# A mixture-of-experts and gated-MLP kernel: fold and scale product a step later, transposes spread through the expert stage

## The chip, the cores and the metric

The kernel runs on one core of a Trainium2 chip. The metric is the time of one execution on the device, in microseconds (us). The core has five engines that work side by side, each through its own queue in order: PE (TensorE, matrix products and transposes into PSUM), DVE (VectorE), ACT (ScalarE), POOL (GpSimd) and SP (SyncE, which issues the DMAs here).

## The reference

Three stages follow each other: an attention between tokens and a few state rows, a soft mixture of experts, and a gated MLP. Cut to what matters here:

```python
attn = concat([softmax(x @ state.T) @ state, softmax(state @ x.T) @ x])   # 8 x 544 rows of 512 = 4352 tokens
logits = attn @ phi                                  # 32 slots: 8 experts with 4 slots each
slot_in = softmax(logits, over tokens).T @ attn
slot_out[e] = relu(slot_in[e] @ w1[e]) @ w2[e]       # 8 experts, 512 -> 1024 -> 512
y = softmax(logits, over slots) @ slot_out           # 4352 x 512
g = y @ w_gate                                       # 512 -> 1536
out = (g * sigmoid(g) * (y @ w_val)) @ w_out         # 1536 -> 512
```

## The kernel before, in words

Every order in it is written by hand: the engines run their instructions in the order in which the Python code emits them.

**Attention stage.** A string of operation names (ORDER) sets it. Neither it nor its code is touched.

**Expert stage** (from L1102). The experts run in two groups g of four. `expert_1` multiplies the slot inputs with w1, `expert_r` applies the relu, `expert_h` transposes the result, `expert_2` multiplies with w2, and `expert_o` copies the outputs out of PSUM (L692) and transposes them by a small product (L694) into the stack ST. Between them lies side work, in generators of which `some(gen, n)` runs n pieces and `run(gen)` the rest. Three `c_calc` (c1, c2, c3) make the softmax over the slots for 16, 16 and 2 blocks of 128 tokens: DVE and ACT up to the exponentials, POOL the scaling and the split into fp16 parts (L609, L619, L622), then PE transposes in groups of eight (L628), each group copied to `cstack` by ACT (L629). `prep_w0` (pg) and `prep_wo0` (pw) convert the first weights. The weights of the MLP come as 64-bit words and are turned to fp32 on the chip by `to32` (L723 POOL or L729 DVE, L725 ACT, L732 and L736 DVE). At L1122 ACT loads the table of the MLP's activation. PSUM has two small banks, s0 and s1, that `psmall` hands out in turn.

**Main stage.** Since y is `cstack` times slot_out, the kernel multiplies the MLP's weights by the slot outputs first ("fold", L847: 32 short products for one pair of 128-wide weight tiles) and never builds y. A step k is one of 102 units: a block of 256 tokens times one weight pair q of six. `front(k)` has four products (L1169) into two of three PSUM banks (`gvp`), an ACT activation (L1170) and a DVE product (L1174) into `sh`; `middle(k)` splits `sh` into two fp16 parts (ACT cast L1182, POOL subtraction L1183) in `hl`; `back(k)` has twelve products (L1219) in two halves into an accumulator, and on a block's last pair each half is scaled out to `osb` (ACT L1231 in the first pass over a block, DVE L1233 later). The loop emits for each k the first half of `back(k)`, `front(k + 3)`, `middle(k + 2)`, and the second half of `back(k)`. As there are three banks and a front takes two, `front(k)` can't write before DVE has read what `front(k - 2)` left: it waits for `sh(k - 2)`. `plan()` decides by LEAD and RATE when the blocks go over from one pair to the next ones.

**Side work of the main stage.** `prep_all` readies the pairs 1 to 5 behind the steps. For a pair: `prep_head` converts two weight tiles (gvf) and folds them (L847, copied by ACT at L857); `prep_mid` converts the third (wof), takes maxima (L800) and joins them with the fold's (L869 to L871) in `mx`; `prep_tail` finds scales: a PE transpose of `mx` (L779), two DVE operations into `D` (L782, L783), a PE product of `D` (L785, the "scale product"), DVE operations on it (L788 to L883), then the folded weights in two fp16 halves (`two`, L890 and L897), which 16 DMAs of SP lay out as `gv` (L902). `spend(bg, credit)` runs after each step: a piece of side work yields its cost or an "S". An "S" ends the side work of that step; otherwise pieces run until the credit is used up. The credit is CN = 2.0, or CR = 1.0 in a block's last step outside the first pass.

Of the kernel before, what the change touches and what calls it, by code (L numbers as in the profile page):

```python
# [32 lines left out]
CC = 0  # L33
NRM = 0, 1
ATD = 1
PA, PB, PC = 0, 0, 0
C2 = 1
# [47 lines left out]
def attn_moe_glu_kernel(  # L85
# [511 lines left out]
    def slot_softmax(src, n, dst):  # L597
        m = sm.tile([128, n], F32, tag="cm", bufs=1, name="cm")
        dve.tensor_reduce(out=m, in_=src, axis=AX.X, op=ALU.max)
        dve.tensor_tensor(out=dst, in0=src, in1=bc(m, NSL), op=ALU.subtract)  # L600
        act.activation(out=dst, in_=dst, func=AF.Exp)
        yield 1.0
        z = sm.tile([128, n], F32, tag="cz", bufs=1, name="cz")
        dve.tensor_reduce(out=z, in_=dst, axis=AX.X, op=ALU.add)
        dve.tensor_scalar(out=z, in0=z, scalar1=EPS, scalar2=None, op0=ALU.add)
        r = sm.tile([128, n], F32, tag="cr", bufs=1, name="cr")
        dve.reciprocal(out=r, in_=z)
        dve.tensor_scalar(out=r, in0=r, scalar1=16384.0, scalar2=None, op0=ALU.mult)
        (pool, dve)[PA].tensor_tensor(out=dst, in0=dst, in1=bc(r, NSL), op=ALU.mult)  # L609
        yield 1.0  # L610

    CT = []

    def c_calc(t0, n):
        c = wk.tile([128, n, NSL], F32, tag=("sp", "so", "edn")[t0 // 16], bufs=1 + t0 // 32, name="cc")
        yield from slot_softmax(Lg[:, t0:t0 + n, :], n, c)
        cc = wk.tile([128, n, 4, NSL], F16, tag=("stn", "C", "edn")[t0 // 16], bufs=1 + t0 // 32, name="cc16")
        for i in range(2):
            pool.tensor_copy(out=cc[:, :, i, :], in_=c) if i >= PB else act.copy(out=cc[:, :, i, :], in_=c)  # L619
        yield 1.0  # L620
# [155 lines left out]
    def scale_bits_slim(mx, n, name):  # L776
# [7 lines left out]
        yield "S"  # L784
# [270 lines left out]
    with tc.manual_schedule():  # L1055
# [87 lines left out]
        expert_2(1, 4, 8)  # L1143
        expert_o(1)
# [128 lines left out]
        for k in range(len(steps)):  # L1273
# [8 lines left out]
            spend(bg, CR if steps[k][5] and steps[k][0][0] else CN)  # L1282
# [63 lines left out]
```

## Time and profile before

| | us |
|---|---|
| median of 3 runs | 467.49 |
| lowest, highest | 465.09, 467.6 |
| the profiled execution: its time | 466.66 |
| its span, first to last instruction | 464.9 |
| attention stage | 0 to about 90 |
| expert stage | about 90 to 129 |
| main stage, first to last L1219 | 136.19 to about 461 |

The profiled execution's time is 1.8 us longer than its span. In the rows, times are us from the start of the span, of a merged row the first start and the time to the last end; a bracket gives the idle time ahead of a row and what ended it.

### The profile page before, as it was taken

The numbers are of one execution on the slowest core, as the hardware profiler recorded it, in microseconds if no ns is written. First come the engines' busy times: TensorE is split into PE (matmuls) and PEld (weight loads), VectorE is DVE, ScalarE is ACT, GpSimd is POOL, SyncE is SP. The second block draws the span as 40 slices with busy tenths as digits, with TensorE's granted clock in tenths as the row PEclk, the third lists the DMA queues.
The fourth block names the chain that finished last, engine by engine and source line by source line (L and its number), as shares of the span: only waits on it lengthen the run. The fifth ranks groups of instructions, "written<-read, shape, count | busy, mean of one in ns | idle before, by whom it ended". The sixth has DMA issues, their size and how long they took to land.

```text
span 464.9 us, 9476 instructions
## 1 busy us (share of the span) xinstructions
PE 441.1 (95%) x3723; PEld 244.9 (53%) x3723; DVE 300.4 (65%) x610; ACT 245.8 (53%) x439; POOL 180.9 (39%) x160
## 2 busy tenths in 40 slices
PE   8789998999988999898999999999999999999997
PEld 6477676544453455454555555555555555555553
DVE  3877988467667786968999878544333334345454
ACT  2678877427348797774655644433344433344440
POOL 0113221072017565644756453333333333333331
PEclk9999999999999899999999999999999999999999
DMA  8999999999999203300000000000011112211224
GB/s 313 421 420 413 413 419 419 390 363 421 419 418 421 87 5 126 155 12 1 1 13 0 7 7 1 13 0 1 1 47 45 47 45 57 80 47 45 90 92 180
DMA packets 19436, 75.04 MB, mean 161 GB/s; under 512 B 5440, under 2 KB 6080, under 8 KB 12608
## 3 DMA queue, kind: packets, MB, share of 16 engines
q1 hardware_dynamic: 19392, 74.45, 40.2%
q8 instruction: 29, 0.48, 0.4%
q14 instruction: 15, 0.12, 0.1%
HBM read 64.87 MB, written 8.91 MB: 159 GB/s over the span
## 4 chain that ended last, share of the span: by engine, by line
PE 70%; DMA 9%; DVE 7%; issue 5%; POOL 5%; ACT 3%; SPq 0%; POOLq 0%; DVEq 0%; ACTq 0%
PE p L1219 44%; PE p L1169 7%; DMA u<-in_wgv_dram 4%; DMA u<-in_xn_dram 4%; PE p L676 3%; POOL hl L1183 3%; PE p L645 3%; PE p L270 2%; POOL u L723 2%; PE p L315 2%; DVE osb L1233 1%; PE s L370 1%; DMA stN<-in_stn_dram 1%; PE s L443 1%; DVE sh L1174 1%
## 5 line engine op out<-in xcount | busy, mean ns | idle before, releaser
L1219 PE MATMUL p<-wo,hl 128*128 128x512 f16 x1014 | 238.2, 381 | 1.8 <-DVE osb L1233 1.7
L1183 POOL TENSOR_TENSOR hl<-sh,hl 128x512 f16<-128x512 f32 x102 | 126.4, 1240 | 191.9 <-ACT hl L1182 188.5
L1219 PEld LDWEIGHTS <-hl 128*128 128x128 f16 x1218 | 118.4, 98 | 123.9 <-issue 4.4
L1174 DVE SCALAR_TENSOR_TENSOR sh<-p,segk,sh 128x512 f32<-128x512 f32 x102 | 76.2, 747 | 85.0 <-ACT sh L1170 83.7
L1170 ACT ACTIVATE sh<-p,sg 128x512 f32<-128x512 f32 x85 | 58.4, 687 | 128.6 <-PE p L1169 128.6
L1182 ACT CAST hl<-sh 128x512 f16<-128x512 f32 x102 | 62.4, 612 | 12.7 <-DVE sh L1174 12.6
L1233 DVE SCALAR_TENSOR_TENSOR osb<-p,segm,osb 128x512 f32<-128x512 f32 x67 | 49.9, 746 | 22.4 <-PE p L1219 22.2
L1219 PE MATMUL p<-bqm,hl 128*128 128x512 f16 x204 | 49.6, 379 | 0.0
L1169 PE MATMUL p<-cstack,gvs 128*128 128x256 f16 x272 | 41.5, 274 | 0.8 <-DVE sh L1174 0.5
L1169 PEld LDWEIGHTS <-gvs 128*128 128x128 f16 x272 | 26.7, 99 | 19.2 <-issue 2.2
L357 POOL TENSOR_TENSOR a<-a,r 128x1024 f32<-128x1024 f32 x7 | 13.4, 1915 | 56.3 <-DVE r L353 17.2
L732 DVE SCALAR_TENSOR_TENSOR u<-u 128x512 uint32<-128x512 uint32 (+1 forms) x33 | 26.4, 809 | 13.4 <-POOL u L723 13.2
L723 POOL TENSOR_SCALAR u<-u 128x512 uint32<-128x512 uint8 x30 | 26.5, 884 | 2.5
L1231 ACT ACTIVATE osb<-p,segk 128x512 f32<-128x512 f32 x28 | 19.2, 692 | 5.2 <-PE p L1219 5.2
L1169 PE MATMUL p<-cstack,gv 128*128 128x256 f16 x136 | 20.4, 273 | 0.0
L736 DVE SCALAR_TENSOR_TENSOR gvf<-gvf,u 128x512 uint32<-128x512 uint32 (+1 forms) x22 | 19.9, 913 | 0.2
L315 PE MATMUL p<-cs,atA 128*128 128x128 f32 x128 | 17.9, 277 | 1.8 <-DVE atA L280 0.5
L1169 PEld LDWEIGHTS <-gv 128*128 128x128 f16 x136 | 13.3, 98 | 8.8
L310 ACT ACTIVATE atA<-atA,nm 128x512 f32<-128x512 f32 x16 | 10.7, 718 | 12.1 <-PE p L315 12.1
L315 PEld LDWEIGHTS p<-cs,atA 128*128 128x128 f32 x128 | 14.3, 140 | 3.6 <-DVE atA L280 1.0
L676 PE MATMUL p<-u,exq 128*32 128x256 f32 x256 | 14.8, 380 | 0.7 <-ACT exq L666 0.7
L725 ACT ACTIVATE gvf<-u 128x512 f32<-128x512 f32 (+1 forms) x22 | 14.8, 722 | 0.0
(214 smaller groups left out, 451.3 us busy)
## 6 DMA issues: line engine op xcount, KB each, us to landing
u<-in_w_dram SPq DMA_DIRECT2D x23, 1024.0 KB, 13.8
u<-in_wgv_dram SPq DMA_DIRECT2D x12, 1024.0 KB, 17.4
u<-in_xn_dram SPq DMA_DIRECT2D x8, 1040.0 KB, 17.9
out_dram<-osb SPq DMA_DIRECT2D x15, 512.0 KB, 2.8
early<-in_w_dram SPq DMA_DIRECT2D x14, 512.0 KB, 9.1
u<-in_wo_dram SPq DMA_DIRECT2D x6, 1024.0 KB, 17.8
u<-in_xt_dram SPq DMA_DIRECT2D x3, 1024.0 KB, 7.3
early<-in_w_dram SPq DMA_DIRECT2D x1, 1024.0 KB, 9.8
```

The lines of the kernel that those rows point to most:

```text
L315: pe.transpose(p[:, j, q * 128:(q + 1) * 128], stsA[:, q, j * 128:(j + 1) * 128], ident)
L676: pe.matmul(out=SO[g][i][32 * j:32 * j + 32, :], lhsT=hT[g, k // 4][:, k % 4, 32 * j:32 * j + 32], rhs=u[:, j, :], start=(k == 0), stop=(k ...
L723: pool.tensor_scalar(out=lo[:, c], in0=byte[:, c], scalar1=2.0 ** -5, scalar2=-31.0 / 64, op0=ALU.mult, op1=ALU.add)
L732: dve.scalar_tensor_tensor(out=lo[:, c], in0=hi[:, c], scalar=0x80000000, in1=lo[:, c], op0=ALU.bitwise_and, op1=ALU.bitwise_or)
L736: dve.scalar_tensor_tensor(out=tu[:, c], in0=tu[:, c], scalar=3, in1=lo[:, c], op0=ALU.logical_shift_left, op1=ALU.bitwise_or)
L1169: pe.matmul(out=p[v][:, 256 * i:256 * i + 256], lhsT=GV[2 * q + i][v], rhs=rhs, start=True, stop=True)
L1170: act.activation(out=sh[:, 0, :], in_=p[0], func=AF.Silu, scale=sgs[q])
L1174: dve.scalar_tensor_tensor(out=sh[:, 1, :], in0=p[1], scalar=(kap0[0] if k == 0 else seg_scale(*seg)[0][q]), in1=sh[:, 0, :], op0=ALU.mult ...
L1182: act.copy(out=t[:, 0, :], in_=sh[:, 1, :])
L1183: pool.tensor_tensor(out=t[:, 1, :], in0=sh[:, 1, :], in1=t[:, 0, :], op=ALU.subtract)
L1219: pe.matmul(out=accs[x], lhsT=t[:, u // 2, c], rhs=WO[2 * q + j][:, u % 2, :], start=first and u == 0 and j == 0, stop=last and (j, u) == ...
L1233: dve.scalar_tensor_tensor(out=o, in0=accs[i], scalar=rsc, in1=o, op0=ALU.mult, op1=ALU.add)
```

## The change

Nothing of the arithmetic is altered. Expert stage: c1's POOL work is done in two halves of eight blocks each, and the transposes of c1 and c2, which stood together after `expert_o(0)`, are spread over `expert_h` and `expert_2`; the new `expert_c` copies an expert group's outputs out of PSUM ahead of the transposes and products that follow. Parts of `prep_w0` come earlier.

Main stage: for pair 1 the fold comes one step later and the conversion of the pair's third tile (`prep_wide`) runs ahead of it; for the pairs 2 to 5 a second "S" puts the scale product and what hangs on it one step later. In steps that are a block's first and last at once, outside the first pass, the credit is CS = 0.7. `plan()` gives 15 steps of the first pass to single blocks where it gave 14, then two blocks with two pairs where it gave three, then six single-pair steps where it gave five; from step 25 on the sequence of segment lengths is as before.

```diff
-LEAD, RATE = 7, 21
-CR = 1.0
+LEAD, RATE = 9, 20
+CR, CS = 1.0, 0.7
 CN = 2.0
-YM = 5
...
-        (pool, dve)[PA].tensor_tensor(out=dst, in0=dst, in1=bc(r, NSL), op=ALU.mult)
-        yield 1.0
-
-    CT = []
+        return r
...
     def c_calc(t0, n):
         c = wk.tile([128, n, NSL], F32, tag=("sp", "so", "edn")[t0 // 16], bufs=1 + t0 // 32, name="cc")
-        yield from slot_softmax(Lg[:, t0:t0 + n, :], n, c)
+        r = yield from slot_softmax(Lg[:, t0:t0 + n, :], n, c)
         cc = wk.tile([128, n, 4, NSL], F16, tag=("stn", "C", "edn")[t0 // 16], bufs=1 + t0 // 32, name="cc16")
-        for i in range(2):
-            pool.tensor_copy(out=cc[:, :, i, :], in_=c) if i >= PB else act.copy(out=cc[:, :, i, :], in_=c)
-        yield 1.0
-        for i in range(2):
-            (pool, dve)[i < PC].tensor_tensor(out=cc[:, :, 2 + i, :], in0=c, in1=cc[:, :, i, :], op=ALU.subtract)
+        CCS[t0] = cc
+        h = 8 if t0 == 0 else n
+        for u in range(0, n, h):
+            v = slice(u, u + h)
+            pool.tensor_tensor(out=c[:, v, :], in0=c[:, v, :], in1=bc(r[:, v], NSL), op=ALU.mult)
+            for i in range(2):
+                pool.tensor_copy(out=cc[:, v, i, :], in_=c[:, v, :])
+            for i in range(2):
+                pool.tensor_tensor(out=cc[:, v, 2 + i, :], in0=c[:, v, :], in1=cc[:, v, i, :], op=ALU.subtract)
         yield 1.0
         for u in range(0, n, 8):
-            k = min(8, n - u)
-            p = psmall([128, 8, 128], F16)
-            for i in range(k):
-                pe.transpose(p[:, i, :], cc[:, u + i, :, :].rearrange("p a s -> p (a s)"), CT[1])
-            (dve.tensor_copy if (u // 8) % 2 < CC else act.copy)(out=CT[0][:, t0 + u:t0 + u + k, :], in_=p[:, :k, :])
+            c_move(t0, u, min(8, n - u), psmall([128, 8, 128], F16))
             yield 1.0
+
+    def c_move(t0, u, k, p):
+        for i in range(k):
+            pe.transpose(p[:, i, :], CCS[t0][:, u + i, :, :].rearrange("p a s -> p (a s)"), CT[1])
+        act.copy(out=CT[0][:, t0 + u:t0 + u + k, :], in_=p[:, :k, :])
...
+    def expert_c(g):
+        for i in range(2):
+            o = wk.tile([128, 256], F32, tag="le", bufs=2, name="so")
+            (dve.tensor_copy if i and g else act.copy)(out=o, in_=SO[g][i])
+            SO[g][i] = o
+
     def expert_p(g, i):
         if i == 0:
             OP[g] = psmall([128, 4, NSL])
-        o = wk.tile([128, 256], F32, tag="le", bufs=2, name="so")
-        (dve.tensor_copy if i and g else act.copy)(out=o, in_=SO[g][i])
+        o = SO[g][i]
...
-            if g:
-                heat(HP_[i], 0)
+        if g:
+            heat(1, 0)
...
-    def scale_bits_slim(mx, n, name):
+    def scale_bits_slim(mx, n, name, steps=1):
         yield "S"
         p = psmall([128, 256])
...
-        yield "S"
+        for _ in range(steps):
+            yield "S"
         pe.matmul(out=p[:, 128:128 + n], lhsT=vb[:n].to_broadcast([n, 128]), rhs=D[:, 0:n], start=True, stop=True)
         yield 0.3
...
-    def prep_head(q):
+    def this_step(gen):
+        n = turn[0]
+        while turn[0] == n:
+            d = next(gen, "S")
+            yield d
+            if d == "S":
+                return
+
+    def prep_head(q, ahead=None):
         yield from conv_gv(2 * q)
         yield from conv_gv(2 * q + 1)
         yield "S"
+        if ahead:
+            yield from this_step(ahead)
         p = psmall([128, 128])
...
-    def prep_mid(q):
+    def prep_wide(q):
         mx = sm.tile([128, 4], F32, tag="mx4", name="mx4")
-        c = conv_wo(q, mx[:, 2:4])
-        for _ in range(YM):
-            yield next(c)
-        wof = yield from c
+        wof = yield from conv_wo(q, mx[:, 2:4])
+        GP["wo", q] = mx, wof
+
+    def prep_mid(q, wide):
+        yield from wide
+        mx, wof = GP.pop(("wo", q))
         r = GP.pop(q)
...
     def prep_tail(q):
         mx, wof, r = GP.pop(q)
-        Q, R = yield from scale_bits_slim(mx, 3, "g")
+        Q, R = yield from scale_bits_slim(mx, 3, "g", 1 + (q > 1))
...
     def prep_all():
-        yield from prep_head(1)
+        wide = prep_wide(1)
+        yield from prep_head(1, wide)
         for q in range(1, NP):
-            yield from prep_mid(q)
+            yield from prep_mid(q, wide if q == 1 else prep_wide(q))
             t, h = prep_tail(q), prep_head(q + 1) if q + 1 < NP else ()
             h = iter(h)
             for d in t:
                 if d != "S":
                     yield d
                     continue
-                n = turn[0]
-                while turn[0] == n:
-                    d = next(h, "S")
-                    yield d
-                    if d == "S":
-                        break
+                yield from this_step(h)
             yield from h
...
-        some(c1, 4)
+        some(c1, 2)
         expert_1(0, 0, 4)
         expert_r(0, 0)
-        some(c2, C2)
+        some(c2, 1)
         expert_1(0, 4, 8)
         free("x")
         expert_h(0, 0)
         expert_r(0, 1)
-        some(c2, 4 - C2)
+        some(c1, 1)
+        some(c2, 1)
+        some(pg, 3)
         expert_2(0, 0, 3)
         expert_h(0, 1)
-        some(c3, 4)
+        some(c1, 1)
+        some(c3, 2)
         expert_2(0, 3, 8)
-        some(pg, 10)
+        expert_c(0)
+        some(c2, 1)
         expert_1(1, 0, 1)
+        some(pg, 7)
         expert_o(0)
         warm = sm.tile([128, 1], F32, tag="warm", bufs=1, name="warm")
         act.activation(out=warm, in_=va, func=AF.Silu)
-        run(c1)
         expert_1(1, 1, 2)
-        run(c2)
+        some(c2, 1)
         expert_1(1, 2, 4)
         expert_r(1, 0)
-        run(c3)
+        some(c3, 1)
         some(pg, 1)
         expert_1(1, 4, 5)
         run(pg)
...
+        expert_c(1)
         expert_o(1)
...
+            seg, _, _, _, first, last = steps[k]
+            spend(bg, (CR, CS)[first] if last and seg[0] else CN)
```

How it moves instructions, at the places that the prediction speaks of. New line numbers are the changed kernel's: L729 is L725 before, L740 is L736, L736 is L732, L872 is L857, L1188 is L1170, L1192 is L1174, L1200 is L1182, L1249 is L1231.

The first fold, on ACT. The fold's result is copied by L857 (L872); the rows around it are ACT's work for steps 3 to 5. Before:

```order
L1231 ACTIVATE osb<-p_2069,segk 128x512
L1170 ACTIVATE sh<-p_1974,s_2012 128x512
L1182 CAST hl<-sh 128x512
L1231 ACTIVATE osb<-p_2070,segk 128x512
L857 COPY bqm<-s_2194 128x128
L725 ACTIVATE wof<-u 128x512 x2
L1231 ACTIVATE osb<-p_2067,segk 128x512
```

Now:

```order
L1249 ACTIVATE osb<-p_2074,segk 128x512
L729 ACTIVATE wof<-u 128x512 x2
L1249 ACTIVATE osb<-p_2071,segk 128x512
L1188 ACTIVATE sh<-p_1980,s_2016 128x512
L1200 CAST hl<-sh 128x512
L1249 ACTIVATE osb<-p_2072,segk 128x512
L872 COPY bqm<-s_2230 128x128
```

The fold, with its copy, went behind one whole step, and the third tile's conversion (wof) ahead of it.

The scale product of pair 2, on DVE: L782 and L783 (now L786 and L787) write what the product on PE reads, L788 (L793) is the first that reads its result. Before:

```order
L782 TENSOR_REDUCE D<-s_2592 3x1
L783 TENSOR_SCALAR D<-cs,D 3x3
L736 SCALAR_TENSOR_TENSOR gvf<-gvf,u 128x512
L1174 SCALAR_TENSOR_TENSOR sh<-p_1975,segk,sh 128x512
L937 RECIPROCAL segm<-MP 128x1
L938 TENSOR_SCALAR segk<-KK,segm 128x1
L939 TENSOR_SCALAR segm<-MP 128x1
L788 TENSOR_SCALAR P<-s_2592 128x3
```

Now:

```order
L786 TENSOR_REDUCE D<-s_2602 3x1
L787 TENSOR_SCALAR D<-cs,D 3x3
L740 SCALAR_TENSOR_TENSOR gvf<-gvf,u 128x512 x2
L1192 SCALAR_TENSOR_TENSOR sh<-p_1979,segk,sh 128x512
L736 SCALAR_TENSOR_TENSOR u<-u 128x512 x2
L740 SCALAR_TENSOR_TENSOR gvf<-gvf,u 128x512
L1192 SCALAR_TENSOR_TENSOR sh<-p_1978,segk,sh 128x512
L793 TENSOR_SCALAR P<-s_2602 128x3
```

Two `sh` products, that is two steps, lie now between writing `D` and reading the scale product, where there was one.

The transposes of the softmax, on ACT in the expert stage: `cstack` is what a group of eight transposes is copied to, `so` the outputs of the first experts, ACT_TABLE_LOAD the table. Before:

```order
L666 COPY exq<-s_1591 128x512
L601 ACTIVATE cc<-cc 128x64
L725 ACTIVATE gvf<-u 128x1024 x2
L692 COPY so<-p_1610 128x256
L692 COPY so<-p_1611 128x256
L703 COPY ST<-s_1737 128x128
L1122 ACT_TABLE_LOAD
L1122 ACTIVATE warm<-cs 128x1
L629 COPY cstack<-s_1749 128x1024
L629 COPY cstack<-s_1759 128x1024
L629 COPY cstack<-s_1773 128x1024
L629 COPY cstack<-s_1783 128x1024
```

Now:

```order
L665 COPY exq<-s_1596 128x512
L629 COPY cstack<-s_1603 128x1024
L729 ACTIVATE gvf<-u 128x1024
L629 COPY cstack<-s_1668 128x1024
L596 ACTIVATE cc<-cc 128x64
L690 COPY so<-p_1630 128x256
L690 COPY so<-p_1631 128x256
L629 COPY cstack<-s_1749 128x1024
L729 ACTIVATE gvf<-u 128x1024
L707 COPY ST<-s_1776 128x128
L1140 ACT_TABLE_LOAD
L1140 ACTIVATE warm<-cs 128x1
```

Three of the four copies to `cstack` that followed the table load stand ahead of it; the fourth is the next instruction behind these.

## Rows read from the trace of the kernel before

**Rows 1.** Stretches: length, busy PE, PEld, DVE, ACT, POOL; PEclk, DMA, GB/s.
```profile
148.53:157.13 8.60, 6.35 (x50) 2.90 (x50) 6.45 (x9) 5.04 (x10) 4.13 (x4) 0.80 0.59 243
157.13:177.42 20.29, 20.29 (x132) 10.46 (x131) 18.05 (x36) 18.30 (x32) 13.30 (x11) 1.00 0.02 5
194.81:231.00 36.19, 34.36 (x207) 17.75 (x207) 30.32 (x61) 20.30 (x36) 18.84 (x15) 1.00 0.02 5
231.00:452.30 221.30, 221.30 (x1224) 114.74 (x1222) 121.90 (x215) 95.87 (x164) 93.73 (x82) 1.00 0.10 34
```

**Rows 2.** Timeline of PE at the first fold: start, length, engine, line, tiles.
```profile
147.24 1.46 PE L1219 MATMUL p<-wo,hl 128*128 128x512 f16 x6
148.62 0.41 PE L847 MATMUL s<-gvf,ST 128*32 128x128 f32 x4
151.29 1.34 PE L847 MATMUL s<-gvf,ST 128*32 128x128 f32 x28 [2.25 <-DVE gvf L736]
152.56 2.74 PE L1219 MATMUL p<-wo,hl 128*128 128x512 f16 x6
```

**Rows 3.** Timeline of DVE in the same stretch.
```profile
147.28 2.70 DVE L732 SCALAR_TENSOR_TENSOR u<-u 128x512 uint32<-128x512 uint32 x2
149.90 0.74 DVE L1174 SCALAR_TENSOR_TENSOR sh<-p,segk,sh 128x512 f32<-128x512 f32 x1
150.56 1.28 DVE L736 SCALAR_TENSOR_TENSOR gvf<-gvf,u 128x512 uint32<-128x512 uint32 x2
151.76 0.74 DVE L1174 SCALAR_TENSOR_TENSOR sh<-p,segk,sh 128x512 f32<-128x512 f32 x1
153.62 0.69 DVE L732 SCALAR_TENSOR_TENSOR u<-u 128x512 uint32<-128x512 uint32 x1 [1.13 <-POOL u L723]
154.85 0.69 DVE L732 SCALAR_TENSOR_TENSOR u<-u 128x512 uint32<-128x512 uint32 x1 [0.54 <-POOL u L723]
```

**Rows 4.** Timeline of POOL in the same stretch.
```profile
147.95 1.48 POOL L1183 TENSOR_TENSOR hl<-sh,hl 128x512 f16<-128x512 f32 x1
151.42 1.43 POOL L1183 TENSOR_TENSOR hl<-sh,hl 128x512 f16<-128x512 f32 x1 [1.99 <-ACT hl L1182]
```

**Rows 5.** Timeline of PE at two later folds and at waits of the main stage.
```profile
175.90 1.59 PE L847 MATMUL s<-gvf,ST 128*32 128x128 f32 x32
...
194.50 0.38 PE L785 MATMUL s<-D,cs 3*128 3x3 f32 x2 [1.41 <-DVE D L783]
...
214.51 1.46 PE L1219 MATMUL p<-wo,hl 128*128 128x512 f16 x6 [0.25 <-DVE osb L1233]
...
219.17 1.02 PE L1219 MATMUL p<-wo,hl 128*128 128x512 f16 x4 [1.48 <-DVE osb L1233]
...
273.32 1.08 PE L847 MATMUL s<-gvf,ST 128*32 128x128 f32 x32
```

**Rows 6.** Timeline of DVE ahead of the wait that ends at 219.17.
```profile
210.30 0.70 DVE L732 SCALAR_TENSOR_TENSOR u<-u 128x512 uint32<-128x512 uint32 x1 [1.68 <-POOL u L723]
...
212.15 1.65 DVE L736 SCALAR_TENSOR_TENSOR wof<-wof,u 128x512 uint32<-128x512 uint32 x1
213.72 0.74 DVE L1233 SCALAR_TENSOR_TENSOR osb<-p,segm,osb 128x512 f32<-128x512 f32 x1
...
218.38 0.74 DVE L1233 SCALAR_TENSOR_TENSOR osb<-p,segm,osb 128x512 f32<-128x512 f32 x1
```

**Rows 7.** Timeline of PE in the expert stage.
```profile
98.34 2.80 PE L676 MATMUL p<-u,exq 128*32 128x256 f32 x48 [0.68 <-ACT exq L666]
...
110.82 0.61 PE L628 MATMUL s<-id,cc 128*128 128x128 f16 x8 [0.81 <-ACT cstack L629]
111.73 0.61 PE L628 MATMUL s<-id,cc 128*128 128x128 f16 x8 [0.31 <-ACT cstack L629]
```

**Rows 8.** Timeline of ACT in the expert stage.
```profile
108.37 1.28 ACT L1122 ACT_TABLE_LOAD   x1
109.67 0.20 ACT L1122 ACTIVATE warm<-cs 128x1 f32<-128x1 f32 x1
109.77 3.74 ACT L629 COPY cstack<-s 128x1024 f16<-128x1024 f16 x4
```

**Rows 9.** DMA issued at 108.06, the experts' last weights: size, us to landing.
```profile
u<-in_w_dram SPq DMA_DIRECT2D x1, 512.0 KB, 17.1
```

**Rows 10.** Chain of waits, the experts' last products: start, length, work.
```profile
124.08 3.20 PE p L676 x56
```

More of the change, by code (lines that the diff above doesn't have):

```diff
@@ L32 @@
 G1 = 5
-CC = 0
 NRM = 0, 1
 ATD = 1
-PA, PB, PC = 0, 0, 0
-C2 = 1
 HT = 2, 2
@@ L41 @@
 H7 = 0
-HP_ = 0, 1
-LEAD, RATE = 7, 21
-CR = 1.0
+LEAD, RATE = 9, 20
+CR, CS = 1.0, 0.7
 CN = 2.0
-YM = 5
 LT = 0, 0
@@ L608, in slot_softmax @@
         dve.tensor_scalar(out=r, in0=r, scalar1=16384.0, scalar2=None, op0=ALU.mult)
-        (pool, dve)[PA].tensor_tensor(out=dst, in0=dst, in1=bc(r, NSL), op=ALU.mult)
-        yield 1.0
-    CT = []
+        return r
+    CT, CCS = [], {}
     def c_calc(t0, n):
         c = wk.tile([128, n, NSL], F32, tag=("sp", "so", "edn")[t0 // 16], bufs=1 + t0 // 32, name="cc")
-        yield from slot_softmax(Lg[:, t0:t0 + n, :], n, c)
+        r = yield from slot_softmax(Lg[:, t0:t0 + n, :], n, c)
         cc = wk.tile([128, n, 4, NSL], F16, tag=("stn", "C", "edn")[t0 // 16], bufs=1 + t0 // 32, name="cc16")
-        for i in range(2):
-            pool.tensor_copy(out=cc[:, :, i, :], in_=c) if i >= PB else act.copy(out=cc[:, :, i, :], in_=c)
-        yield 1.0
-        for i in range(2):
-            (pool, dve)[i < PC].tensor_tensor(out=cc[:, :, 2 + i, :], in0=c, in1=cc[:, :, i, :], op=ALU.subtract)
+        CCS[t0] = cc
[7 more added lines that the diff above has]
+                pool.tensor_tensor(out=cc[:, v, 2 + i, :], in0=c[:, v, :], in1=cc[:, v, i, :], op=ALU.subtract)
         yield 1.0
         for u in range(0, n, 8):
-            k = min(8, n - u)
-            p = psmall([128, 8, 128], F16)
-            for i in range(k):
-                pe.transpose(p[:, i, :], cc[:, u + i, :, :].rearrange("p a s -> p (a s)"), CT[1])
-            (dve.tensor_copy if (u // 8) % 2 < CC else act.copy)(out=CT[0][:, t0 + u:t0 + u + k, :], in_=p[:, :k, :])
+            c_move(t0, u, min(8, n - u), psmall([128, 8, 128], F16))
             yield 1.0
+    def c_move(t0, u, k, p):
+        for i in range(k):
+            pe.transpose(p[:, i, :], CCS[t0][:, u + i, :, :].rearrange("p a s -> p (a s)"), CT[1])
+        act.copy(out=CT[0][:, t0 + u:t0 + u + k, :], in_=p[:, :k, :])
     hT, SO, HP = {}, {}, {}
@@ L1281, in attn_moe_glu_kernel @@
                 seg_scale(*seg)
-            spend(bg, CR if steps[k][5] and steps[k][0][0] else CN)
+            seg, _, _, _, first, last = steps[k]
+            spend(bg, (CR, CS)[first] if last and seg[0] else CN)
 _OUTS = [((B * ROWS, DM), "float32")]
```

## Prediction

> **What bounds the kernel now.** I read the stretches of the execution first, then the engines' timelines where PE stands still. From 231.00 to 452.30 PE is busy for 221.30 of 221.30 us at the full granted clock [rows 1]. Of its 1224 instructions 64 are two folds of 1.08 us each, as at 273.32 [rows 5], and the rest goes by 16 to a step: (221.30 - 2.16) / (1160 / 16) = 3.02 us a step. Nothing waits for another engine there, and the change keeps the number of steps, so nothing is to be had behind 231. What can move lies ahead of it, in three places: the first fold, two waits near 194 and 219, and the expert stage.
>
> At the first fold PE waits 2.25 us for DVE to finish the second weight tile [rows 2]. Then the granted clock falls for a while: the mean is 0.80 in the stretch, and six products that took 1.46 us at 147.24 take 2.74 us at 152.56, half speed, the 1.2 GHz level [rows 1, 2]. Fold and step 4 together take 8.60 us [rows 1] and would take 3.02 + 1.08 = 4.10 undisturbed: 4.50 us are lost.
>
> **The fold a step later.** The work is the same, with its place in PE's queue changed, so I follow PE by the old times. Step 4 starts at 148.53. Its first half, six products, takes 1.29 us, the time from 147.24 to 148.53, and ends at 149.82. `front(7)` may write once DVE has read sh(5), at 149.90 + 0.74 = 150.64 [rows 3]: a new wait of 0.8 us, which the fold's wait hid. With 3.02 - 2 x 1.29 = 0.44 for the front and 1.29 for the second half PE comes to the fold at 152.37. The second tile is ready at 150.56 + 1.28 = 151.84 [rows 3], so the fold does not wait and ends at 153.45, where it ended with step 4 at 157.13: 3.68 us gained there.
>
> What is late next is DVE, which has no less work than before. From 148.53 to 177.42, where the second fold ends, it stands idle for 8.60 - 6.45 + 20.29 - 18.05 = 4.39 us [rows 1], and it can come earlier only by these. Of them 1.13 + 0.54 = 1.67 us were waits for POOL's share of the third tile [rows 3]; POOL gets to it only behind the subtraction that ends at 151.42 + 1.43 = 152.85 [rows 4], with the old order and with the new one. That leaves 4.39 - 1.67 = 2.7 us. The second fold took 1.59 us instead of 1.08 [rows 5], so it was held up by DVE already, and PE cannot leave it sooner than DVE lets it. I take **2.7 us** for this term. The likely place where PE waits instead is the transpose L779 in step 7, which needs DVE's `mx`. The upper end is 3.68 + 0.51 = 4.2, when DVE's waits vanish too.
>
> The lower end comes from DVE beside POOL. Two L732 that ran beside POOL's subtraction took 2.70 us, two L736 of the same size without one 1.28 [rows 3, 4]: 0.7 us more for each that meets one. With less idle time three more of the twelve conversions ahead of the second fold may meet one: 2.7 - 2.1 = 0.6. The Trainium skill (SBUF — State Buffer, section Who interferes with whom) says that a DVE instruction with two SBUF inputs and a GpSimd instruction that reads SBUF shut each other out for the whole instruction. The trace agrees, with 2.70 us against 1.28; were all twelve to meet a subtraction, the page's rule would leave nothing of this term, which speaks against the change.
>
> **The scale product a step later.** For pair 2 it waits 1.41 us for DVE's `D` [rows 5]. By the order, a second `sh` product now lies between, so PE comes a whole step, 3.02 us, later, more than twice the wait. The pieces that follow (`two`, 16 DMAs) come later too, but `plan()` gives the second pair a step later, and the side work of pair 2 still ends ahead of the front that reads it. Term: 0 to 1.4, taken **1.3**. The cover is DVE's own speed: if DVE is slower by a step, the wait is back.
>
> **Fewer conversions in one-pair steps.** In such a step DVE has two evictions and a product, 0.74 us each [rows 6], so about 0.8 of 3.02 us is left for side work. PE waited 0.25 and 1.48 us for evictions [rows 5]; the stretch has 36.19 - 34.36 = 1.83 us of idle PE in all [rows 1]. DVE was late since it first waited 1.68 us for POOL, then ran a conversion of 1.65 us beside it, ahead of the eviction [rows 6]. Now the conversions start two steps behind the fold, not one, and a maximum and what follows it go to later steps. The wait for POOL and the conversion ahead of an eviction stay as such. I take **1.2**, ends 0.3 and 1.8. `plan()` itself costs nothing: 102 steps either way.
>
> **The expert stage.** PE waits 0.68 us for a copy, 0.81 and 0.31 us for ACT's copies to `cstack` [rows 7]; the latter two stand behind the table load, 1.28 us, and in a row of four, 3.74 us [rows 8]. One group of transposes, 0.61 us [rows 7], now fills the first wait, and only one copy of a group is left behind the load. That is 0.61 + 0.81 + 0.31 = 1.73 us. POOL's work in halves is hidden, as its first half is due only at the first group, and the copies of `so` go by while PE transposes. A floor is the last weights: they land at 108.06 + 17.1 = 125.2 [rows 9], and PE needed them for the last 8 of the 56 products from 124.08 on, at 124.08 + 48/56 x 3.20 = 126.8 [rows 10]: 1.6 to 1.7 us earlier and no more. Taken **1.6**, ends 1.0 (a copy of the hidden layer delayed by the conversion that is now ahead of it on DVE) and 1.8. The Trainium skill (ScalarE: Activation LUTs, section What ACT_TABLE_LOAD costs) puts 1.38 us of drain behind the load's 1.28; here the next ACT instruction starts at 109.67, 0.02 us after the load's end [rows 8]. By the page the copy left behind the load would be later by that and this term smaller by an estimated 0.3.
>
> **The sum.** 2.7 + 1.3 + 1.2 + 1.6 = 6.8 us, against the profiled execution's own time: 466.66 - 6.8 = **459.9 us**. The ends add up to 0.6 + 0 + 0.3 + 1.0 = 1.9 (464.8) and 4.2 + 1.4 + 1.8 + 1.8 = 9.2 (457.5). The median of the runs, 467.49, lies 0.8 above the profiled execution and the lowest 1.6 below; I make no correction.
>
> **Rivals.** *DVE sets the pace.* Conversions and subtractions get into each other's way as soon as PE stands still less, and the terms of the main stage are given back wait by wait. For it: DVE is busy for 18.05 of 20.29 us, ACT for 18.30, POOL for 13.30 ahead of the second fold [rows 1]. Against it: DVE has 4.39 us idle. Only the expert stage and 0.3 are left: 466.66 - 1.9 = 464.8.
>
> *DVE keeps up.* All ends are met: 457.5. For it: part of DVE's 4.39 us was idle since PE stood or ran at half speed, and that part goes by itself. Against it: the 1.67 us that wait for POOL.
>
> *The clock falls again,* and the kernel is slower. A wait of 2.25 us with the fall behind it cost 2.25 + (157.13 - 152.56 - 3.02) = 3.8 us [rows 1, 2]. If DVE comes more than 2.25 us late at the L779 of step 7, at the second fold and at the scale product of pair 2, that makes 3 x 3.8 = 11.4 against 4.5 + 0.5 of the first and second fold and 1.6 of the experts: 466.66 + 4.8 = 471.5. It decides from a wait of 2.25 us on; the waits of 1.41 and 1.48 us [rows 5] had no fall behind them, as the stretch 194.81 to 231.00 has the clock at 1.00 [rows 1].
>
> *The expert term isn't there,* since the last weights come no sooner than PE takes them: 461.5.
>
> **How the numbers follow.** Chances: forecast 0.60, DVE keeps up 0.16, DVE sets the pace 0.16, clock 0.05, no expert term 0.03. The range of 8 in 10 takes in the upper end and half a microsecond beyond it, as runs of one kernel differ by that, and stops short of DVE setting the pace: 457.0 to 464.4. A measurement of this kernel can tell about 0.5%, 2.3 us, from no change. DVE setting the pace gains 1.9, mostly within that: faster 0.60 + 0.16 + 0.03 + 0.04 = 0.83, same 0.12, slower 0.05.
>
> **What would show it.** Right: the first fold without a wait and the clock at 1.00 to the end; PE idle between 0.5 and 1.0 us at `front(7)`; a wait under 1.5 us at L779 or the second fold; none at the scale product of pair 2; the last stretch unchanged at 3.02 us a step; the first L1219 about 1.6 us earlier, at 134.6. Wrong: a granted clock under 1 after 130 us; waits of PE for `D`, `gvf` or `osb` of over 3 us in sum; the first L1219 later than 135.5; a front that waits for the DMAs of `gv`.

## The result and the profile after

The changed kernel takes **471.25 us** (median of 5 runs, 470.67 to 472.12) against 467.49: ratio 1.009, 95% interval 1.0061 to 1.0119, so 2.9 to 5.6 us slower. The forecast was 459.9. The profiled execution took 470.67 us (span 468.9).

To see where the time went, I compare the start of the same step in both traces. The first instruction of a step on ACT is its Silu (L1170 before, L1188 after); there are 102 in each, and their numbers count from 0. Timeline of ACT after, the Silu of steps 0, 30, 38, 39, 48, 51 and 101:

```profile
132.16 0.69 ACT L1188 ACTIVATE sh<-p,s 128x512 f32<-128x512 f32 x1 [0.35 <-PE p L1187]
...
228.52 0.69 ACT L1188 ACTIVATE sh<-p,sg 128x512 f32<-128x512 f32 x1 [1.83 <-PE p L1187]
...
254.86 0.69 ACT L1188 ACTIVATE sh<-p,sg 128x512 f32<-128x512 f32 x1
...
260.06 0.69 ACT L1188 ACTIVATE sh<-p,sg 128x512 f32<-128x512 f32 x1 [3.35 <-PE p L1187]
...
288.83 0.69 ACT L1188 ACTIVATE sh<-p,sg 128x512 f32<-128x512 f32 x1 [0.34 <-PE p L1187]
...
304.87 0.69 ACT L1188 ACTIVATE sh<-p,sg 128x512 f32<-128x512 f32 x1 [2.25 <-PE p L1187]
...
456.20 0.69 ACT L1188 ACTIVATE sh<-p,sg 128x512 f32<-128x512 f32 x1 [1.83 <-PE p L1187]
```

| step | before | after | after - before |
|---|---|---|---|
| 0 | 133.46 | 132.16 | -1.30 |
| 30 | 233.91 | 228.52 | -5.39 |
| 38 | 259.87 | 254.86 | -5.01 |
| 39 | 262.89 | 260.06 | -2.83 |
| 48 | 291.77 | 288.83 | -2.94 |
| 51 | 300.85 | 304.87 | +4.02 |
| 101 | 452.19 | 456.20 | +4.01 |

By step 30 the changed kernel is 5.4 us ahead, where 6.8 were forecast. (0.3 of it is only put off: the scale product of pair 3 ran ahead of step 30 before, at 228.78, and runs behind it now, at 229.87.) It loses 0.4 us by step 38, then 2.2 us in one step, 7.0 us in three, and nothing behind them. The view of stretches between the Silus of steps 30, 38, 39, 48, 51 and 101, after (columns as in [rows 1]):

```profile
228.52:254.86 26.34, 26.07 (x165) 13.45 (x163) 26.10 (x45) 15.13 (x26) 13.86 (x13) 1.00 0.03 6
254.86:260.06 5.20, 3.30 (x20) 1.59 (x18) 5.13 (x11) 1.30 (x2) 2.52 (x4) 1.00 0.00 0
260.06:288.83 28.77, 28.77 (x181) 15.04 (x179) 20.95 (x39) 14.95 (x26) 14.51 (x13) 1.00 0.03 5
288.83:304.87 16.04, 12.39 (x54) 5.73 (x52) 10.13 (x22) 3.69 (x6) 4.36 (x4) 0.79 0.01 2
304.87:456.20 151.33, 151.33 (x803) 78.28 (x801) 65.56 (x104) 61.23 (x103) 57.85 (x50) 1.00 0.13 47
```

In the second stretch PE stands still for 5.20 - 3.30 = 1.90 us; in the fourth for 16.04 - 12.39 = 3.65 us, and the granted clock is 0.79. In the last row of [rows 1] there was neither. Timeline of PE after; L852, L783 and L790 are the fold L847, the transpose L779 and the scale product L785 of before:

```profile
149.38 0.60 PE L1187 MATMUL p<-cstack,gvs 128*128 128x256 f16 x4 [0.60 <-DVE sh L1192]
...
151.20 1.08 PE L852 MATMUL s<-gvf,ST 128*32 128x128 f32 x32
...
160.12 0.27 PE L783 MATMUL s<-cs,mx 128*3 128x128 f32 x1 [1.61 <-DVE mx L888]
...
172.85 1.59 PE L852 MATMUL s<-gvf,ST 128*32 128x128 f32 x32
...
187.49 0.27 PE L783 MATMUL s<-cs,mx 128*3 128x128 f32 x1 [0.84 <-DVE mx L888]
...
193.74 0.38 PE L790 MATMUL s<-D,cs 3*128 3x3 f32 x2
...
258.18 0.27 PE L783 MATMUL s<-cs,mx 128*3 128x128 f32 x1 [1.90 <-DVE mx L888]
...
288.79 1.46 PE L1237 MATMUL p<-bqm,hl 128*128 128x512 f16 x6
293.90 0.37 PE L783 MATMUL s<-cs,mx 128*3 128x128 f32 x1 [3.65 <-DVE mx L888]
294.06 2.77 PE L1237 MATMUL p<-wo,hl 128*128 128x512 f16 x6
```

Both losses are waits of the transpose for `mx`: of pair 4 at 258.18, of pair 5 at 293.90. Behind the second one six products take 2.77 us in place of 1.46, the 1.2 GHz level. The loss of 7.0 us is the 3.65 us of the wait, 0.4 us for the transpose and the scale product of pair 5, which ran ahead of step 48 before (at 283.42 and 286.65) and run behind it now, and the other 2.9 us are half speed.

Why is `mx` of pair 5 late? DVE's timeline in the kernel before, from the second conversion step of pair 5's output weight to `mx`, with the transpose on PE, and ahead of them the POOL subtraction behind which the conversion begins:

```profile
273.25 1.16 POOL L1183 TENSOR_TENSOR hl<-sh,hl 128x512 f16<-128x512 f32 x1 [1.87 <-ACT hl L1182]
...
276.43 0.69 DVE L732 SCALAR_TENSOR_TENSOR u<-u 128x512 uint32<-128x512 uint32 x1 [0.54 <-POOL u L723]
277.03 0.69 DVE L736 SCALAR_TENSOR_TENSOR wof<-wof,u 128x512 uint32<-128x512 uint32 x1
...
282.37 0.23 DVE L870 TENSOR_SCALAR mx<-cs,mr 128x2 f32<-128x2 f32 x1
282.51 0.15 DVE L871 TENSOR_TENSOR mx<-mx 128x1 f32<-128x1 f32 x1
...
283.42 0.27 PE L779 MATMUL s<-cs,mx 128*3 128x128 f32 x1
```

The same of the changed kernel, with the fold of pair 5 on PE ahead of it and POOL's subtractions L1201 below it:

```profile
273.93 1.08 PE L852 MATMUL s<-gvf,ST 128*32 128x128 f32 x32
...
284.20 0.69 DVE L736 SCALAR_TENSOR_TENSOR u<-u 128x512 uint32<-128x512 uint32 x1 [0.55 <-POOL u L727]
284.81 1.65 DVE L740 SCALAR_TENSOR_TENSOR wof<-wof,u 128x512 uint32<-128x512 uint32 x1
...
288.36 0.14 DVE L946 TENSOR_REDUCE segm<-MP 128x1 f32<-128x3 f32 x1
288.54 0.17 DVE L950 RECIPROCAL segm<-segm 128x1 f32<-128x1 f32 x1
288.74 1.01 DVE L951 TENSOR_SCALAR segk<-KK,segm 128x3 f32<-128x3 f32 x1
289.78 0.15 DVE L952 TENSOR_SCALAR segm<-segm 128x1 f32<-128x1 f32 x1
289.85 0.68 DVE L740 SCALAR_TENSOR_TENSOR wof<-wof,u 128x512 uint32<-128x512 uint32 x1
...
292.60 1.09 DVE L887 TENSOR_SCALAR mx<-cs,mr 128x2 f32<-128x2 f32 x1
293.60 0.15 DVE L888 TENSOR_TENSOR mx<-mx 128x1 f32<-128x1 f32 x1
...
281.02 1.16 POOL L1201 TENSOR_TENSOR hl<-sh,hl 128x512 f16<-128x512 f32 x1 [1.87 <-ACT hl L1200]
...
284.25 1.66 POOL L1201 TENSOR_TENSOR hl<-sh,hl 128x512 f16<-128x512 f32 x1
288.56 1.15 POOL L1201 TENSOR_TENSOR hl<-sh,hl 128x512 f16<-128x512 f32 x1 [2.65 <-ACT hl L1200]
292.51 1.15 POOL L1201 TENSOR_TENSOR hl<-sh,hl 128x512 f16<-128x512 f32 x1 [2.79 <-ACT hl L1200]
```

Before, `mx` was ready at 282.66, 0.76 us ahead of PE. From the start of the first row to the end of `mx` it took 6.23 us then and takes 9.55 now, 3.32 more: a conversion that meets a subtraction, 0.96 (1.65 for 0.69); the four `segk` operations, which used to stand behind `mx`, 1.49; the product L887 that meets a subtraction, 0.86 (1.09 for 0.23). And PE comes 1.1 us sooner, 5.88 us after that start (288.79 + 1.29 = 290.08, behind the six products) in place of 6.99. The conversion begins behind a subtraction of POOL, at 273.25 before and at 281.02 now. Before, the fold of pair 5 (1.08 us, at 273.32 [rows 5]) stood between that subtraction and the transpose; now it runs at 273.93, two steps ahead of the subtraction. 3.32 + 1.11 - 0.76 = 3.67: the wait.

`mx` of pair 4 meets a subtraction in the same two places. Timeline of DVE after:

```profile
250.64 1.66 DVE L740 SCALAR_TENSOR_TENSOR wof<-wof,u 128x512 uint32<-128x512 uint32 x1
...
253.48 1.27 DVE L805 TENSOR_REDUCE mx<-wof 128x1 f32<-128x512 f32 x2
...
256.95 1.02 DVE L887 TENSOR_SCALAR mx<-cs,mr 128x2 f32<-128x2 f32 x1
```

The conversion and L887 cost 0.97 and 0.79 us more than alone, and pair 4 had no slack in the kernel before (its rows stand in the section on why the prediction was wrong).

### The profile page after: what moved, and what is told of

It reads as the page before. It is cut to its first block, busy times and chain, and to the rows that moved or that the text cites. A ratio compares the mean times of both kernels' runs of the same rounds, so it can differ in the third digit from the quotient of the medians.

```text
span 468.9 us, 9480 instructions
## 1 busy us (share of the span) xinstructions
PE 443.6 (95%) x3723; PEld 246.5 (53%) x3723; DVE 309.3 (66%) x612; ACT 246.3 (53%) x439; POOL 181.4 (39%) x165
## 4 chain that ended last, share of the span: by engine, by line
PE 71%; DVE 11%; issue 6%; DMA 5%; POOL 4%; ACT 3%; SPq 0%; DVEq 0%; ACTq 0%; POOLq 0%
PE p L1237 44%; PE p L1187 7%; DMA u<-in_xn_dram 4%; PE p L644 3%; PE p L675 3%; POOL hl L1201 2%; PE p L265 2%; POOL u L727 2%; DVE wof L740 2%; PE p L310 2%; DVE sh L1192 2%; DVE osb L1251 1%; PE s L365 1%; DMA stN<-in_stn_dram 1%; PE s L852 1%
## 5 line engine op out<-in xcount | busy, mean ns | idle before, releaser
L1201 POOL TENSOR_TENSOR hl<-sh,hl 128x512 f16<-128x512 f32 x102 | 126.7, 1242 | 196.2 <-ACT hl L1200 190.1
L1192 DVE SCALAR_TENSOR_TENSOR sh<-p,segk,sh 128x512 f32<-128x512 f32 x102 | 76.2, 747 | 81.3 <-ACT sh L1188 80.1
L1188 ACT ACTIVATE sh<-p,sg 128x512 f32<-128x512 f32 x85 | 58.4, 687 | 127.5 <-PE p L1187 127.5
L1200 ACT CAST hl<-sh 128x512 f16<-128x512 f32 x102 | 62.4, 612 | 23.9 <-DVE sh L1192 23.0
L1251 DVE SCALAR_TENSOR_TENSOR osb<-p,segm,osb 128x512 f32<-128x512 f32 x69 | 51.4, 746 | 23.9 <-PE p L1237 23.7
L736 DVE SCALAR_TENSOR_TENSOR u<-u 128x512 uint32<-128x512 uint32 (+1 forms) x33 | 27.2, 843 | 12.4 <-POOL u L727 12.3
L1249 ACT ACTIVATE osb<-p,segk 128x512 f32<-128x512 f32 x30 | 20.5, 689 | 2.8 <-PE p L1237 2.8
L740 DVE SCALAR_TENSOR_TENSOR gvf<-gvf,u 128x512 uint32<-128x512 uint32 (+1 forms) x22 | 21.3, 985 | 0.1
L729 ACT ACTIVATE gvf<-u 128x512 f32<-128x512 f32 (+1 forms) x22 | 15.2, 723 | 0.0
```

Of the source, the lines that this page charges most:

```text
L736: dve.scalar_tensor_tensor(out=lo[:, c], in0=hi[:, c], scalar=0x80000000, in1=lo[:, c], op0=ALU.bitwise_and, op1=ALU.bitwise_or)
L740: dve.scalar_tensor_tensor(out=tu[:, c], in0=tu[:, c], scalar=3, in1=lo[:, c], op0=ALU.logical_shift_left, op1=ALU.bitwise_or)
L1188: act.activation(out=sh[:, 0, :], in_=p[0], func=AF.Silu, scale=sgs[q])
L1192: dve.scalar_tensor_tensor(out=sh[:, 1, :], in0=p[1], scalar=(kap0[0] if k == 0 else seg_scale(*seg)[0][q]), in1=sh[:, 0, :], op0=ALU.mult ...
L1200: act.copy(out=t[:, 0, :], in_=sh[:, 1, :])
L1201: pool.tensor_tensor(out=t[:, 1, :], in0=sh[:, 1, :], in1=t[:, 0, :], op=ALU.subtract)
```

## The experiments

**Theory A:** the loss behind step 38 is these two waits (and the half speed behind the second), and it is the place of pairs 4 and 5's side work that makes them: too few steps between conversion and transpose. **Rivals:** VectorE has no time left, and a wait that is removed comes back elsewhere (B); one part alone is guilty (credit D, moved fold F, planner I).

**Give the transposes of pairs 4 and 5 a step more** (`e1_mx_late`), at the end of `prep_mid`:
```
+        if q > 3:
+            yield "S"
         GP[q] = mx, wof, r
```


> The transpose of mx goes one step (3.02 us) later for pairs 4 and 5; all else as in the changed kernel. Theory A (the loss is two waits of TensorE at that transpose, 1.90 us at 258.18 and 3.65 us at 293.90, the second with a fall of the granted clock behind it): a step covers the first wait wholly and leaves some 0.6 us of the second, without a fall. The changed kernel gave away 2.4 us round the first and 6.4 us round the second against the kernel before (starts of the same step in both traces), so 470.7 - 2.4 - 5.8 = 462.5 us. Rival B (VectorE as a whole is behind, and the wait comes back at the next place that wants it, the scale product or the evictions): 467 us or more, with a new wait of over 1.5 us behind 255. Rival C (the front that needs pair 4 or 5 now waits for its weights): a wait at the front's matmuls behind 300 us.


Measured: 463.65 us (462.44 to 465.52), ratio 0.9925 (0.9903 to 0.9948). Both waits are gone, pair 5's by little (`mx` is ready at 293.32). Timeline of PE, the transposes of pairs 4 and 5:
```profile
260.76 0.27 PE L783 MATMUL s<-cs,mx 128*3 128x128 f32 x1
...
293.47 0.27 PE L783 MATMUL s<-cs,mx 128*3 128x128 f32 x1
```
Theory A holds, B and C fall: one empty step in two places makes the slower kernel faster than the kernel before. The meetings with POOL are still there (L740 1.64, L887 1.09 us ahead of the second transpose); nobody waits for them now.

**Take the extra step of the scale product back** (`e2_no_extra_step`):
```
-        Q, R = yield from scale_bits_slim(mx, 3, "g", 1 + (q > 1))
+        Q, R = yield from scale_bits_slim(mx, 3, "g")
```


> The scale product of pairs 2 to 5 is put back to the step behind the transpose; all else as in the changed kernel. Theory A, with the extra step as what moved the later folds away from their conversions: the fold of pair 5 stands again in the step of its output weight's conversion, so TensorE comes 1.08 us later to the transpose than in the changed kernel; the four segk operations (1.45 us) still stand ahead of mx. The kernel before had 0.76 us to spare there, so a wait of 0.7 to 1.6 us, no fall; at pair 4 a wait of 0 to 1; the wait of 1.4 us at the scale product of pair 2 is back. 470.7 - 2.4 - 6.4 + 1.0 + 0.5 + 1.4 = 464.8 us. Rival D (the credit of one-pair steps makes mx late, not the extra step): the two waits stay, 470 to 472 us.


Measured: 464.82 us, ratio 0.9964 (0.994 to 0.9988). Pair 4's wait is gone, pair 5's is 1.24 us without a fall of the clock. The scale product waits 0.28 us in pair 2 and 1.09 in pair 3.

**Take the smaller credit back** (`e3_credit_1`):
```
-CR, CS = 1.0, 0.7
+CR, CS = 1.0, 1.0
```


> The credit of one-pair steps is 1.0 again, not 0.7; all else as in the changed kernel. By the order the fold and the conversion of pair 5 come into one step (41) and the transpose into step 44; pair 4 has three steps from the conversion to the transpose, as now, with the fold ahead of them. Theory A: the wait of pair 5 falls from 3.65 to 0.7 to 1.6 us and loses its fall of the clock, that of pair 4 stays near 1.9, and up to 1.2 us of waits for evictions near 200 to 220 come back: 470.7 - 5.4 + 0.6 = 465.9 us, 464.5 to 467. Rival D (the credit alone makes mx late): both waits go, 461 to 462. Rival E (the credit has nothing to do with it): 470 to 472.


Measured: 466.3 us, ratio 0.9987 (0.9965 to 1.0009). Pair 5 does not wait: nothing that stands ahead of its `mx` on DVE takes over 1 us (L951 and L887 take 0.23 again). Pair 4 still does, and this time with a fall of the clock behind it:
```profile
255.28 0.27 PE L783 MATMUL s<-cs,mx 128*3 128x128 f32 x1 [1.97 <-DVE mx L888]
255.39 2.61 PE L1237 MATMUL p<-wo,hl 128*128 128x512 f16 x6
```
So pair 4's wait comes from the extra step, and pair 5's long one takes the extra step and the credit together. D is half true, and only for pair 5; E falls.

**Put the first fold back** (`e4_fold_back`):
```
-        yield from prep_head(1, wide)
+        yield from prep_head(1)
```


> The first fold is put back ahead of the conversions of pair 1's output weight; from step 6 on the order is that of the changed kernel. Theory A (the moved fold has no part in the late waits): both waits at the transposes of pairs 4 and 5 stay, and what the moved fold gave by step 10, 3.1 - 1.3 = 1.8 us, is lost: 472.5 us, 471.5 to 473.5. Rival F (the moved fold makes VectorE's work tighter for the rest of the main stage and so causes the late waits): 464 to 467 us.


Measured: 472.75 us, ratio 1.0125 (1.0083 to 1.0167). PE waits 2.25 us at the first fold again, 1.25 at pair 4 (less than the 1.90 of the changed kernel, which I had not expected), 3.64 at pair 5. F falls.

**All five transposes a step later** (`e5_mx_late_all`; the `yield "S"` of the first run without its `if`):


> The transpose of mx goes a step later for all five pairs. In the run with pairs 4 and 5 alone (463.65 us) TensorE still waited 1.61 us at pair 1's transpose and 0.80 us at pair 2's. Theory A (each of these waits is a matter of how many steps lie between the conversion and the transpose): both go, 463.65 - 2.4 = 461.2 us, 460.3 to 462.3. Rival B (VectorE has no time to give; the waits come back at sh, osb or D): 463 to 465 us, with new waits of over 2 us in sum between 160 and 300 us.


Measured: 463.52 us, ratio 0.9929 (0.9901 to 0.9957): no better than pairs 4 and 5 alone, so my 461.2 was wrong. No transpose waits, but pair 1's scale product, which has no extra step, does, and the granted clock falls behind it (four products of the front take 1.06 us in place of 0.60); the weights of two pairs come too late to their fronts:
```profile
167.25 0.38 PE L790 MATMUL s<-D,cs 3*128 3x3 f32 x2 [1.82 <-DVE D L787]
...
169.03 1.06 PE L1188 MATMUL p<-cstack,gvs 128*128 128x256 f16 x4
...
184.85 0.27 PE L1188 MATMUL p<-cstack,gvs 128*128 128x256 f16 x1 [0.58 <-DMA gvs<-two]
...
218.13 0.27 PE L1188 MATMUL p<-cstack,gv 128*128 128x256 f16 x1 [0.86 <-DMA gv<-two]
```
Here rival B is right: ahead of step 30 DVE has little to give, and a wait that is pushed comes back.

**The four `segk` operations behind the side work** (`e6_segk_behind`; `seg_scale(*seg)` moved below `spend(...)`):


> In a step the four segk operations are written behind the side work, not ahead of it; all else as in the changed kernel. They took 1.45 us ahead of mx of pair 5. Theory A: pair 5's wait at the transpose falls from 3.65 us to about 2.2, pair 4's (whose segk operations stand in a step without other side work) stays at 1.9. The half clock behind pair 5's wait cost 6.4 - 3.65 = 2.8 us: if the shorter wait has the fall behind it too, 471.25 - 1.45 = 469.8 us; if not, 467.0. Rival H (the segk operations are hidden behind waits for GpSimd and cost nothing): 471 us and a wait of 3.5 us or more.


Measured: 469.89 us, ratio 1.0059 (1.0029 to 1.009). Pair 5's wait is 2.68 us, not 2.2, with the fall of the clock behind it. The operations still stand ahead of `mx`, but no longer beside a subtraction, and take 0.71 us for 1.49. So their meeting with POOL was the larger half of their price; I was wrong to count all of it as gone, and H falls.

**The expert stage's part alone** (`e7_expert_only`; the four lines of the main stage as before: numbers 7, 21 and 1.0, no extra step, no `wide` at the first fold):


> The kernel before with the expert stage's part alone; from the first step of the main stage on its order is that of the kernel before. By the two traces this part brings the first main product from 136.19 to 134.88, 1.3 us. If the rest runs as in the kernel before: 467.46 - 1.3 = 466.2 us, ratio 0.997. Rival (the earlier start meets the weights' transfers or the clock, and the 2.25 us wait at the first fold grows by as much): ratio 1.000.


Measured: 465.96 us, ratio 0.9983 (0.9959 to 1.0006): by itself it can't be told from no change, though the middle is a gain of 0.8. The rival's longer wait isn't there: at the first fold PE waits 2.26 us. The trace is sharper: from the first product of the expert stage to the first main product it took 136.19 - 90.01 = 46.18 us before, and 136.55 - 91.98 = 44.57 here.

**The planner's numbers back** (`e8_plan_back`):
```
-LEAD, RATE = 9, 20
+LEAD, RATE = 7, 21
```


> The planner's two numbers are put back (7 and 21), all else as in the changed kernel. By the order the transposes of pairs 4 and 5 stand in the same steps (36 and 46) with the same work ahead of them. Theory A (the planner has no part in it): both waits stay, 470 to 472.5 us. Rival I (the planner's shift of the one-pair steps caused the late waits): under 467 us.


Measured: 470.39 us, ratio 1.0063 (1.004 to 1.0086); waits of 1.90 and 3.64 us stay. I falls.

**The extra step for pairs 2 and 3 only** (`e11_extra_step_23`; `1 + (q in (2, 3))`):


> The scale product's extra step stays for pairs 2 and 3 and is taken from pairs 4 and 5; all else as in the changed kernel. By the order pair 4's transpose and what stands ahead of it are as in the changed kernel, and pair 5's fold comes back into the step of its conversion (42, transpose in 45). Theory A: pair 4's wait stays at 1.9 us; pair 5's falls from 3.65 to 0.7 to 1.3 us, without a fall of the clock: 471.25 - 5.5 = 465.7 us, 464.8 to 466.8; from the first to the last Silu 324.05 - 5.5 = 318.5 us. Rival J (pair 5 is late for what was left over from pair 4, not for its own fold and conversion): a wait of 3 us or more and 470 to 472 us.


Measured: 464.89 us, ratio 0.995 (0.9927 to 0.9973). Pair 4's wait stays (1.89 us), pair 5's is gone. DVE ahead of it, POOL's subtraction beside the conversion, and the transpose:
```profile
280.72 0.69 DVE L740 SCALAR_TENSOR_TENSOR wof<-wof,u 128x512 uint32<-128x512 uint32 x1
...
282.37 0.23 DVE L951 TENSOR_SCALAR segk<-KK,segm 128x3 f32<-128x3 f32 x1
...
286.78 0.23 DVE L887 TENSOR_SCALAR mx<-cs,mr 128x2 f32<-128x2 f32 x1
...
281.08 1.35 POOL L1201 TENSOR_TENSOR hl<-sh,hl 128x512 f16<-128x512 f32 x1 [1.00 <-ACT hl L1200]
...
287.21 0.27 PE L783 MATMUL s<-cs,mx 128*3 128x128 f32 x1
```
The four `segk` operations are ahead of `mx` here too, the fold is back in the conversion's step, and no operation of DVE is held up: where the conversion at 280.72 overlaps a subtraction, it is the subtraction that takes longer, 1.35 us for 1.16. So there is no wait, where I had expected 0.7 to 1.3 us, but no slack either (`mx` is ready at 287.06). J falls; pair 5's lateness is made by its own fold, conversion and meetings. And since pair 4 still waits here and not in e2, its wait comes from the extra step of an earlier pair, 2 or 3, not from its own.

**Two versions meant to be faster:** the transposes of pairs 2, 4 and 5 later with the planner at 7, 21 (`e9_late245_plan`), and of pairs 4 and 5 with 7, 21 (`e10_late45_plan`).


> The transpose of mx a step later for pairs 2, 4 and 5, and the planner's two numbers back to 7 and 21. From the first Silu of the main stage to the last one the run with pairs 4 and 5 late took 316.32 us (the kernel before 318.72, the changed one 324.05); the planner's numbers alone, put back, stood 0.8 us better by step 30; pair 2's wait was 0.80. Theory A: 316.32 - 0.8 - 0.8 = 314.7 us for that stretch, no wait at a transpose but pair 1's 1.6, and 462.0 us in all. Rival B (the waits come back elsewhere): 316 to 317 us for the stretch, 463.5 us or more.

> The transpose a step later for pairs 4 and 5 only, with the planner's numbers back to 7 and 21. Theory A: 316.32 - 0.8 = 315.5 us from the first to the last Silu, 462.8 us in all. Rival (the 0.8 us by step 30 were the place of pair 2's 0.8 us wait and come back with it): 316.3 us, 463.6 us in all.


Measured: 463.66 us, ratio 0.9922 (0.9891 to 0.9952), and 463.18 us, 0.9922 (0.9895 to 0.9948). They beat the kernel before, but in whole time they can't be told from e1. From Silu 0 to Silu 101 e9 takes 315.27 us and e10 314.98, where the kernel before has 318.72, the changed one 324.05 and e1 316.32. (In e10's profile the granted clock is 0.50 from 130 to 135 us, so its span can't be compared in whole, and its step 0 is late: from there to step 2 it takes 3.18 us, where e9 has 3.73. From step 2 to step 101 e9 takes 311.54 us and e10 311.80.) So e10 did what Theory A expected. e9 missed its 314.7 by 0.6 us, with a new wait of 0.40 us for `gvf` at the fold of pair 4, and its whole time is the one that rival B had. Pair 2's later transpose adds nothing that the whole time shows.

## Why the prediction was wrong

**The step that failed** is the first part's conclusion: "Nothing waits for another engine there ... so nothing is to be had behind 231", and with it the unchanged last stretch. The rows were read rightly, but a PE that is busy for 221.30 of 221.30 us shows that nobody is late, not by how little. The slack stood in the same trace: pair 5's `mx` was ready 0.76 us ahead of the transpose, and pair 4's with nothing to spare (timelines of DVE and PE before):
```profile
254.25 0.15 DVE L871 TENSOR_TENSOR mx<-mx 128x1 f32<-128x1 f32 x1
...
254.55 0.27 PE L779 MATMUL s<-cs,mx 128*3 128x128 f32 x1
```
`mx` ends at 254.40, 0.15 us ahead of the transpose. Where the transpose does wait it starts no sooner: after, `mx` of pair 5 ends at 293.75 and the transpose starts at 293.90. So 0.15 us is no slack. Two of the edits act on every pair from 2 on, and I followed them for pair 2 only. That costs 2.2 + 7.0 us.

**Expert stage:** forecast 1.6; 44.58 for 46.18 us in the changed kernel (134.88 - 90.30), 1.60. Right. The first main product came at 134.88 and not at 134.6 since the stage began 0.29 us later.

**The moved fold:** forecast 2.7, ends 0.6 to 4.2. By step 10 the changed kernel is 3.1 us ahead, 1.3 of them already at step 0, so the fold gave 1.8; the run with the fold back (e4) is 1.6 us slower by step 30, each from its step 0. The first fold doesn't wait and `front(7)` waits 0.60, as forecast; the transpose in step 7 waits 1.61, a little over the 1.5 that I allowed, and the second fold still takes 1.59. DVE limits more than I took; a conversion that meets a subtraction costs 0.96 us more (1.65 for 0.69), where I took 0.7.

**The scale product:** forecast 1.3 from pair 2. Its wait is gone. Without the extra step it would have been 0.28 in pair 2 and 1.09 in pair 3, so most of the gain came from the pair that I hadn't looked at: 1.8 us by step 30 (e2 against the changed kernel, each from its step 0). It was paid for with pairs 4 and 5.

**The credit:** forecast 1.2; 0.7 by step 30 (e3). **The planner's numbers:** forecast free; 0.8 us lost by step 30 (e8).

**The sum ahead of step 30:** forecast 6.8, found 1.6 + 4.1 = 5.7, less the 0.3 of the later start: 5.4. So the terms that the text worked out were about right in sum, in part by luck: those of the main stage were each off by 0.5 to 0.9, not all the same way. The one that it set to nothing decided.

**The rivals:** "The clock falls again" named the mechanism (a transpose that waits for `mx`, with half speed behind it) and 471.5 us. It had its places in step 7, the second fold and pair 2's scale product: there the one wait was 1.61 us, in step 7, with the clock at 1.00 behind it. Its time agrees by accident. "DVE sets the pace" is what e5 shows, ahead of step 30.

**The Trainium skill's rule** in the fold's term (SBUF — State Buffer, Who interferes with whom) was weighed at the wrong place. The same section of the Trainium skill says that a `tensor_scalar` in the modes that use both ports can be shut out by GpSimd as well; the trace agrees that a `tensor_scalar` is held up, with L887 at 1.09 us beside the subtraction and 0.23 without. Which mode L887 runs in no run shows.

## What to carry to other kernels

An engine that is busy all the time says nothing of how close the others run behind it: before a change of order is costed, read for each later repeat of the pattern how long ahead of its use the result was ready, and take off what lies between the two even where the consumer waits (0.15 us here). An edit in a generator that serves all pairs has to be followed for all pairs, in the order that comes out. And of two cures, moving the consumer one step costs nothing where steps are free, and comes back as another wait where they aren't (e1 against e5).

## What the runs showed of the hardware

A DVE operation on 128 x 2 values took 0.23 us alone and 1.09 us beside a subtraction of POOL that had begun 0.09 us sooner, and ended with it (293.69, POOL 293.66): held up by the other's length, not its own. Where DVE's conversion began first, the subtraction took longer (e11: 1.35 us for 1.16). Two reductions from 253.48 on, beside a subtraction from 253.74 to 254.90, took 1.27 us, 0.64 each, no more than one alone (0.68).

The granted clock fell behind waits of PE of 1.82 (e5), 1.97 (e3), 2.25 [rows 2], 2.68 (e6) and 3.65 us; behind waits of 1.61, 1.86 (e6), 1.89 (e11) and 1.90 us it stayed at 1.00. So the prediction's "from a wait of 2.25 us on" was too high, and the length of a wait alone doesn't decide.

In unchanged code ahead of the experts the profiles differ: the first expert product came at 90.01 us in the profile before and between 90.0 and 92.1 in the twelve others. The granted clock differs there too: the changed kernel has 0.83 from 10 to 20 us, e2 has 0.83 from 20 to 30 us, and the kernel before has 1.00 in both. That is why the parts are compared from step 0 on, not by whole spans.
